# A fused RWKV and ELU-MLP kernel: a planner's order of work replaced by written-out lines for each engine

## The chip, the cores and the metric

The kernel runs on one core of a Trainium2 chip. A core has five engines that take their instructions in order, each from its own line, and wait for one another by semaphores: TensorE (PE in the profile; PEld is its weight load), VectorE (DVE), ScalarE (ACT), GpSimd (POOL) and SyncE (SP), which here only issues DMAs. The metric is the device time of one launch in microseconds (us), lower is better.

## The reference

For 4 batches and 8 heads of width 48 a state of 48x48 runs over 768 steps: the output row of a step is r_t (state + (u k_t) v_t), and then the state becomes w_t state + k_t v_t. The rows of all heads, 384 wide, 3072 of them, go through an MLP with a hidden width of 2048:

```python
for t in range(S):
    cur = np.einsum('bhd,bhe->bhde', u[None] * kt, vt)
    y[:, :, t] = np.einsum('bhd,bhde->bhe', rt, state + cur)
    state = wt[:, :, :, None] * state + np.einsum('bhd,bhe->bhde', kt, vt)
...
h = x @ w_in
g = np.where(h > 0.0, h, alpha * (np.exp(np.minimum(h, 0.0)) - 1.0))
return (g @ w_out).astype(np.float32)
```

## The kernel before, in words

**Attention.** The recurrence is cut into 24 units of 512 token rows over all heads (six chunks of four units). Units 0 to 3 hold 128 steps of one batch, the others 64 steps of two batches. A unit i is a set of tasks, named by a letter code and i:

- `ld_w`, `ld_k`, `ld_rk`, `ld_v`: its loads (SP). `es`, `gs` (L488, L497 and L498, VectorE): running products of the decays w. `rh` (L503): k and r times those. `rk`, `rku`, `md` (L510, L513, L517): the diagonal term. `sp` puts it into a mask tile `ams` (ScalarE L545, VectorE L550 or, from unit 8, GpSimd L556).
- `tr` (L590) transposes k on TensorE, `kt` (L636, ScalarE) copies it out. `s` (L590, L597) makes the scores in PSUM, `mk` (L626 to L632, VectorE) puts them into `ams`. `v` (L577, L648) makes the unit's output and its part of the state; from unit 8 (the stacked units) `v` runs first the scores of unit i + 1 (L597), then the state part (L648), then the outputs (L577, into py).
- `rc`, `tc`: four DMAs each that put r and the state into the tiles of a stacked unit (SP, L567 and L573). `xf`, `xh`, `xl`: the unit's output split into two fp32r halves. `up`, `sc` (L705, L640): update and scaling of the state. `fl` (L507, ScalarE) counts decays over 1 (for units 0 to 7 on a second load of w, `ld_wx`, into the one buffer `wx`); `pc` (L493) keeps the unit's product of decays. `least`, `guard`, `verdict` make a check of the two at the end.

**MLP.** The 16 slices f of the hidden width arrive as 64-bit floats and are converted once: `raw` (load), `a`, `cs` (ScalarE), `cb`, `cc` (VectorE L735, L739), `wh`, `wl` (L742 to L754, the two fp32r halves). For a chunk and a slice there is a step n (104 in all; numbers run through the chunks, 24 in the first, which also has steps of a quarter and half of the columns in plain fp32, then 16 in each): `g1.n` (TensorE, L303 or L299: 9 or 6 matmuls into `ph`), `r1.n`, `r2.n` (ScalarE L307, L310), `stt.n` (VectorE L313), `gh.n` (ScalarE L317), `gl.n` (VectorE L321), `g2.n` (TensorE, L334 or L331, into `acc`). `ph`, `m`, `gh` and `gl` have two buffers each. `out`, `store` bring out a chunk; at the end `g2a`, `part` and `end.0` to `end.3` do it in pieces.

**The order.** `Plan` holds each task with its engine, a duration (`COST`), the tasks it follows (`after`) and the buffers it takes (`hold`). `Plan.order` is a list scheduler: it steps through time and gives each free engine the ready task with the earliest due time, worked back from the due times of the chunks (`BEGINS`) and shifted by a table of amounts for single tasks (`NUDGE`); a task marked `lock` on VectorE or GpSimd isn't started while a locked one runs on the other engine. The tasks are then emitted in the planned order, which fixes each engine's line; at run time only semaphores hold an instruction back. Up to `g2.0` some matmuls on a tile of ones (`FILL`, L457) are put in front of named tasks.

Of the kernel before, what the change touches and what calls it, by code (L numbers as in the profile page):

```python
# [22 lines left out]
NC = S // C  # L23
# [20 lines left out]
DUE = {0: 9.0}  # L44
# [18 lines left out]
COST = dict(es=1.235, gs=1.47, pc=0.2, pd=0.9, md=0.165, spa=2.43, spd=0.685, rh=0.685, hat=1.22, rk=0.48, rku=0.48, prk=1.02, prku=1.02, dg=0.545, mk=0.74, mk0=1.4, up=0.545, upa=0.32,  # L63
            sc=0.6, xl=0.557, cand=0.555, cv=0.955, wl=0.952, stt=0.688, gl=0.69, fl=0.93, kt=0.522, xh=0.48, a=0.905, sg=2.0, la=0.913, wh=0.833, wg=0.83, r1=0.598, r2=0.632,
            gh=0.62, sp=1.95, s=1.62, s0=1.6, s8=0.82, tr=0.42, v=1.7, v0=1.6, v9=2.3, vs=0.47, vu=0.37, mk2=1.5, drc=300, dtc=300, g=2.04, g32=2.65, out=0.6)
# [10 lines left out]
FIRST = "ACT"  # L76
SPARE = (1,)
PAD = 32
RAW_AT = (1.6, 1.6)
LEAD = 110.0  # L80
# [1035 lines left out]
```

## Time and profile before

| | us |
|---|---|
| median of 3 runs | 503.06 (502.89 to 504.56) |
| the profiled execution | 502.57 |
| its span (first to last instruction) | 500.9 |
| TensorE busy | 488.9 (98%) |
| VectorE busy | 350.0 (70%) |
| ScalarE busy | 270.6 (54%) |
| GpSimd busy | 41.4 (8%) |

Busy is the time in which an engine has an instruction under way. Matmuls overlap, and the profile draws each longer than the distance to the next one, so a short stop of TensorE can lie under a drawn matmul.

### The profile page before, as it was taken

To read this page: it belongs to the slowest core of one execution; us is meant where nothing else is said; L and a number is where in the kernel's file an instruction comes from. 1 tells how busy PE (TensorE), PEld (TensorE's weight loads), DVE (VectorE), ACT (ScalarE), POOL (GpSimd) and SP (SyncE) were. 2 spreads that over 40 slices of the span, in tenths; PEclk is the share of its full clock that TensorE was granted. 3 is DMA by queue.
4 is the path that set the end of the run, shared out by engine and by line. 5 is a ranking of instruction groups with operands and counts; after the bars stand their busy time and mean duration, and the time that the engine had idled before them with its cause. 6 is when DMAs were issued, how large, how long until landed. Compare 5 with 4: busy or idle time off the path is not lost.

```text
span 500.9 us, 12029 instructions
## 1 busy us (share of the span) xinstructions
PE 488.9 (98%) x5014; PEld 403.0 (80%) x5014; DVE 350.0 (70%) x525; ACT 270.6 (54%) x526; POOL 41.4 (8%) x57
## 2 busy tenths in 40 slices
PE   9998999999999999998999999999999999999996
PEld 8986888777887888886887778878888878888885
DVE  7999999989998997444899463699564343333332
ACT  4986677656654635535565625437445253544542
POOL 2000000002233011010011020020111000000000
PEclk9999999999999999999999999999999999999999
DMA  8999266634624543335951427032430100010001
GB/s 272 348 286 299 61 227 190 213 94 112 195 50 111 146 130 92 118 92 132 210 151 50 142 64 198 22 106 84 109 100 6 28 3 1 0 65 0 1 0 67
DMA packets 45611, 57.27 MB, mean 114 GB/s; under 512 B 29168, under 2 KB 29296, under 8 KB 45552
## 3 DMA queue, kind: packets, MB, share of 16 engines
q1 hardware_dynamic: 45120, 55.66, 39.7%
q8 instruction: 41, 0.67, 0.6%
q10 hardware_dynamic: 432, 0.79, 0.4%
q14 instruction: 18, 0.15, 0.1%
HBM read 45.42 MB, written 4.72 MB: 100 GB/s over the span
## 4 chain that ended last, share of the span: by engine, by line
PE 62%; DVE 18%; DMA 10%; issue 4%; ACT 3%; SPq 2%; DVEq 0%; ACTq 0%
PE ph L303 27%; PE acc L334 25%; DMA wraw<-in_wraw_dram 5%; DMA wx<-in_wkr_dram 3%; PE acc L331 2%; DMA k<-in_wkr_dram 2%; DVE gl L321 2%; DVE m L313 2%; PE py L577 2%; DVE k L503 2%; PE ph L299 2%; DVE eg L488 2%; DVE ams L632 1%; PE px L597 1%; DVE w_l L754 1%
## 5 line engine op out<-in xcount | busy, mean ns | idle before, releaser
L313 DVE SCALAR_TENSOR_TENSOR m<-m,ph 128x512 f32<-128x512 f32 (+2 forms) x104 | 66.6, 641 | 74.7 <-ACT m L310 74.5
L303 PE MATMUL ph<-xh,w_l 128*128 128x512 f32 x270 | 105.5, 391 | 0.8 <-DVE w_l L754 0.8
L334 PE MATMUL acc<-gh,w_l 128*128 128x512 f32 x268 | 104.6, 390 | 0.0
L307 ACT ACTIVATE m<-ph 128x512 f32<-128x512 f32 (+2 forms) x104 | 58.4, 563 | 80.0 <-PE ph L303 65.3
L321 DVE TENSOR_TENSOR gl<-m,gh 128x512 fp32r<-128x512 f32 x90 | 62.2, 692 | 43.9 <-ACT gh L317 43.8
L317 ACT CAST gh<-m 128x512 fp32r<-128x512 f32 x90 | 55.6, 618 | 66.5 <-PE acc L334 40.0
L303 PE MATMUL ph<-xh,w_h 128*128 128x512 f32 x180 | 72.2, 401 | 1.2 <-DVE m L313 1.1
L334 PE MATMUL acc<-gl,w_h 128*128 128x512 f32 x180 | 70.5, 392 | 1.5 <-DVE gl L321 1.5
L334 PE MATMUL acc<-gh,w_h 128*128 128x512 f32 x180 | 71.7, 398 | 0.0
L303 PE MATMUL ph<-xl,w_h 128*128 128x512 f32 x180 | 70.2, 390 | 0.0
L310 ACT ACTIVATE m<-m 128x512 f32<-128x512 f32 (+2 forms) x104 | 62.1, 599 | 2.1
L303 PEld LDWEIGHTS ph<-xh,w_l 128*128 128x128 f32 x270 | 50.7, 188 | 12.0 <-DVE w_l L754 1.2
L334 PEld LDWEIGHTS acc<-gh,w_l 128*128 128x128 f32 x268 | 50.3, 188 | 10.4
L556 POOL TENSOR_SCALAR_AFFINE_SELECT ams<-md 64x512 f32<-64x512 f32 x32 | 28.4, 887 | 217.1 <-PE py L577 178.9
L334 PEld LDWEIGHTS acc<-gl,w_h 128*128 128x128 f32 x180 | 33.8, 188 | 9.4 <-DVE gl L321 2.8
L303 PEld LDWEIGHTS ph<-xh,w_h 128*128 128x128 f32 x180 | 33.8, 188 | 9.3 <-DVE m L313 1.6
L334 PEld LDWEIGHTS acc<-gh,w_h 128*128 128x128 f32 x180 | 33.8, 188 | 8.1 <-ACT gh L317 0.4
L303 PEld LDWEIGHTS ph<-xl,w_h 128*128 128x128 f32 x180 | 33.8, 188 | 6.5
L303 PE MATMUL ph<-xh,w_g 128*128 128x512 f32 x90 | 35.5, 394 | 0.5 <-DVE m L313 0.5
L303 PE MATMUL ph<-xl,w_g 128*128 128x512 f32 x90 | 35.0, 389 | 0.0
L334 PE MATMUL acc<-gh,w_g 128*128 128x512 f32 x88 | 34.9, 397 | 0.0
L334 PE MATMUL acc<-gl,w_g 128*128 128x512 f32 x88 | 34.6, 393 | 0.2
(121 smaller groups left out, 683.8 us busy)
## 6 DMA issues: line engine op xcount, KB each, us to landing
wraw<-in_wraw_dram SPq DMA_DIRECT2D x16, 768.0 KB, 9.7
k<-in_wkr_dram SPq DMA_DIRECT2D x24, 448.0 KB, 5.1
rk<-in_rk_dram SPq DMA_DIRECT2D x20, 384.0 KB, 4.3
w<-in_wkr_dram SPq DMA_DIRECT2D x24, 227.9 KB, 4.1
wide<-in_vp_dram SPq DMA_DIRECT2D x32, 128.0 KB, 3.6
out_dram<-o SPq DMA_DIRECT2D x15, 256.0 KB, 2.7
ams<-k SPq DMA_DIRECT2D x64, 48.0 KB, 2.4
wide<-st SPq DMA_DIRECT2D x64, 48.0 KB, 2.1
```

Source lines behind the costliest of these rows:

```text
L299: nc.tensor.matmul(ph, w_f[f][:, 0, k], x_[2][:, k], start=(k == 0), stop=(k == NK - 1))
L303: nc.tensor.matmul(ph, w[f][:, 0, k], y[:, k], start=(k == n == 0), stop=(k == NK - 1 and n == 2))
L307: act(s["m"], s["ph"], AF.Relu, scale=-1.0)
L310: act(s["m"], s["m"], AF.Exp, scale=-1.0)
L313: stt_(s["m"], s["m"], -1.0, s["ph"], ALU.add, ALU.max)
L317: nc.scalar.copy(s["gh"], s["m"])
L321: nc.vector.tensor_tensor(s["gl"], s["m"], s["gh"].bitcast(F32), ALU.subtract)
L331: nc.tensor.matmul(a_, w_f[f][:, 1, m], fold(s, s["m"][:, a:b]), start=first, stop=final)
L334: nc.tensor.matmul(a_, w[f][:, 1, m], fold(s, g[:, a:b]), start=(first and n == 0), stop=(final and n == 2))
L488: nc.vector.tensor_tensor_scan(out=eg[:, 0, 0:n][:, ::-1], data0=u_["w"][:, 1:n + 1][:, ::-1], data1=reset[:, 0, 0:n][:, ::-1], initial=0. ...
L503: tt(t, t, u_["eg"][:, :, 0:u_["n"]].rearrange("d z (s t) -> d z s t", t=u_["L"] + 1)[..., 1:], ALU.mult)
L556: nc.gpsimd.affine_select(out=am[rs, h].rearrange("t q p s -> t (q p) s"), in_=u_["md"][rs].rearrange("t q p -> t (q p)").unsqueeze(2).bro ...
```

## The change

`Plan.order` no longer chooses. `SEQUENCE` holds a written-out line of all tasks for each engine and for SP; `order` walks these lines with the task durations and merges them into one emission order. `NUDGE`, the due times and the locks go; some `COST` entries and load sizes are set anew, which now affects only how the lines are merged. The task `v` of a stacked unit becomes two: `va` (scores of the next unit and the state part) and `v` (the outputs); `mk` of the next unit and `up` follow `va`, and the bank px is given free after it. The instructions of all tasks stay. The diff, cut (all of PE's line, the start of the others):

```diff
-DUE = {0: 9.0}
...
-BEGINS = (21.0, 114.0, 191.0, 266.5, 342.0, 417.5, 483.5)
-SOON = 0.0
-SLACK = 1.0
-EARLY = 8.0
-STAG = 17.0
-STAG1 = 9.0
...
+SEQUENCE = dict(
+    PE="""
+pd.0 s.0 pd.1 s.1 v.0 v.1 g1.0 g1.1 pd.2 g1.2 g2.0 g1.3 g2.1 s.2 g2.2 g1.4 v.2 pd.3 g1.5 g2.3 g2.4 s.3 g1.6 g2.5 g1.7 v.3 g2.6 g1.8 g2.7 g1.9 g1.10
+g2.8 g1.11 g2.9 g1.12 g2.10 g1.13 g2.11 g1.14 g2.12 s.4 g2.13 g1.15 g1.16 v.4 g2.14 g1.17 g1.18 g2.15 g2.16 g1.19 s.5 g2.17 g1.20 v.5 g2.18 g2.19 s.6
+g1.21 v.6 g2.20 g1.22 s.7 g2.21 v.7 g1.23 g2.22 g1.24 g1.25 g2.23 g1.26 g1.27 g2.24 g2.25 g1.28 g1.29 g2.26 tr.8 g2.27 g1.30 s.8 g1.31 g2.28 g2.29
+va.8 v.8 g1.32 g1.33 tr.9 g2.30 g1.34 va.9 v.9 g2.31 g2.32 g2.33 g1.35 tr.10 g1.36 va.10 v.10 g2.34 g1.37 g2.35 tr.11 g1.38 g1.39 g2.36 va.11 v.11
+g2.37 g1.40 g1.41 tr.12 g2.38 g2.39 g1.42 va.12 v.12 g1.43 g2.40 tr.13 g2.41 g1.44 g1.45 g2.42 g2.43 g1.46 g2.44 g1.47 g1.48 g2.45 g1.49 va.13 v.13
+g2.46 g2.47 g1.50 tr.14 g2.48 va.14 v.14 g1.51 g1.52 g2.49 g1.53 tr.15 g2.50 g2.51 g1.54 g1.55 va.15 v.15 g2.52 g2.53 g1.56 g1.57 tr.16 g2.54 g2.55
+g1.58 va.16 v.16 g1.59 g2.56 g1.60 g2.57 tr.17 g1.61 g2.58 g1.62 va.17 v.17 g2.59 g2.60 g1.63 tr.18 g2.61 va.18 v.18 g1.64 g1.65 g2.62 tr.19 g2.63
+g1.66 g1.67 g2.64 g1.68 g2.65 g2.66 va.19 v.19 g1.69 g1.70 g2.67 g1.71 g2.68 g1.72 g2.69 g2.70 tr.20 g1.73 g2.71 g1.74 va.20 v.20 g1.75 g2.72 g2.73
+g1.76 g1.77 g2.74 g1.78 g2.75 g1.79 g2.76 g2.77 g1.80 g1.81 tr.21 g2.78 g1.82 g2.79 g2.80 g1.83 va.21 v.21 g2.81 g1.84 g2.82 g1.85 g2.83 g1.86 g1.87
+va.22 v.22 g2.84 v.23 g2.85 g1.88 g2.86 g2.87 g1.89 g1.90 g2.88 g1.91 g1.92 g2.89 g2.90 g1.93 g1.94 g2.91 g2.92 g1.95 g1.96 g2.93 g1.97 g2.94 g1.98
+g2.95 g1.99 g2.96 g2.97 g1.100 g1.101 g2.98 g2.99 g1.102 g1.103 g2.100 g2.101 g2a.0 guard g2a.1 g2a.2 g2.102 g2.103
+""",
+    DVE="""
+es.0 gs.0 rkc.0 es.1 rh.0 gs.1 rkc.1 mk.0 cb.2 rh.1 cc.2 cb.0 cc.0 mk.1 cb.1 cc.1 xl.0 cb.3 rkc.2 es.2 stt.0 gs.2 stt.1 rh.2 es.3 stt.2 cc.3 stt.3
+mk.2 gs.3 rkc.3 cb.6 cb.4 stt.4 rh.3 es.4 cc.4 cc.6 cb.5 stt.5 cc.5 mk.3 stt.6 wl.6 es.5 stt.7 cb.7 gs.4 cb.8 cc.7 stt.8 rk.5 cc.8 wl.7 stt.9 rk.4
+sc.4 rku.4 wl.8 stt.10 gs.5 md.4 xl.2 stt.11 xl.3 cb.9 rku.5 xl.1 stt.12 cc.9 sp.4 rh.4 cb.10 stt.13 md.5 cc.10 wl.9 stt.14 mk.4 rk.6 gl.14 wl.10 es.6
+cb.11 stt.15 cc.11 gs.6 stt.16 gl.15 sc.5 sp.5 xl.4 cb.12 rk.7 rku.6 cc.12 gl.16 wl.11 stt.17 rh.5 up.4 cb.13 md.6 stt.18 gl.17 wl.12 cc.13 stt.19
+rh.6 mk.5 sc.6 gl.18 wl.13 cb.14 gl.19 sp.6 cc.14 up.5 xl.5 rku.7 es.7 stt.20 md.7 mk.6 sp.7 gl.20 wl.14 gs.7 sc.7 xl.6 up.6 rh.7 stt.21 cb.15 gl.21
+cc.15 rk.8 mk.7 stt.22 wl.15 rku.8 gl.22 md.8 es.8 xl.7 gs.8 stt.23 up.7 es.9 rk.10 gl.23 rk.9 stt.24 rh.8 stt.25 rku.9 gl.24 sc.8 gl.25 es.10 wl.0
+gs.10 rku.10 stt.26 stt.27 sc.9 gl.26 gl.27 gs.9 md.10 md.9 stt.28 wl.2 wl.1 stt.29 gl.28 rk.11 gl.29 rh.9 mk.8 rh.10 stt.30 es.11 gs.11 wl.3 stt.31
+gl.30 gl.31 xl.8 up.8 sc.10 mk.9 stt.32 rk.12 es.12 gl.32 stt.33 rh.11 rku.12 gs.12 stt.34 rku.11 gl.33 wl.4 md.12 es.13 xl.9 md.11 up.9 wl.5 sc.11
+mk.10 gl.34 gs.13 stt.36 stt.35 gl.35 gl.36 rk.13 rk.14 xl.10 up.10 stt.37 sc.12 rku.14 rh.12 gl.37 mk.11 es.14 stt.38 rku.13 md.13 gs.14 md.14 xl.11
...
+    ACT="""
+pc.0 md.0 pc.1 sp.0 a.2 cs.2 kt.0 a.0 cs.0 md.1 sp.1 a.1 cs.1 kt.1 xf.0 up.0 xh.0 a.3 cs.3 r1.1 xf.1 up.1 r1.0 r2.0 md.2 r2.1 sp.2 r1.2 r1.3 r2.2 r2.3
+a.6 pc.3 kt.2 cs.6 a.4 cs.4 r1.4 xf.2 pc.2 up.2 r2.4 md.3 sp.3 cs.5 a.5 r1.5 r2.5 wh.6 kt.3 a.7 r1.6 r2.6 xh.2 cs.7 r1.7 r2.7 a.8 xf.3 cs.8 xh.1 r1.8
+r2.8 pc.4 wh.7 r1.9 r2.9 cs.9 wh.8 r1.10 xh.3 r2.10 cs.10 r1.11 r2.11 a.9 r1.12 r2.12 up.3 r1.13 a.10 r2.13 wh.9 r1.14 r2.14 pc.5 wh.10 gh.14 kt.4
+a.11 cs.11 r1.15 r2.15 r1.16 pc.6 r2.16 gh.15 cs.12 fl.0 xh.4 a.12 r1.17 gh.16 r2.17 wh.11 cs.13 r1.18 a.13 r2.18 wh.12 gh.17 gh.18 r1.19 r2.19 wh.13
+a.14 kt.5 gh.19 cs.14 xh.5 r1.20 cs.15 r2.20 fl.1 wh.14 pc.7 kt.6 gh.20 r1.21 xh.6 a.15 r2.21 gh.21 r1.22 r2.22 kt.7 wt.0 wh.15 gh.22 xh.7 r1.23 r2.23
...
+    SP="""
+ld_w.0 ld_k.0 ubd ld_w.1 raw.2 ld_k.1 raw.0 raw.1 ld_v.0 ld_v.1 raw.3 ld_k.2 ld_w.2 ld_w.3 ld_v.2 raw.6 raw.4 ld_k.3 ld_v.3 ld_w.4 raw.5 raw.7 ld_w.5
+raw.8 ld_rk.4 raw.9 ld_rk.5 ub raw.10 ld_k.4 ld_v.4 ld_w.6 ld_rk.6 ld_k.5 raw.11 ld_rk.7 ld_v.6 raw.12 ld_wx.0 raw.13 ld_k.6 ld_v.5 ld_v.8 ld_k.7
+raw.14 ld_w.7 ld_wx.1 ld_v.7 raw.15 ld_w.8 ld_rk.8 ld_wx.2 ld_v.9 ld_w.9 ld_k.8 ld_rk.9 ld_rk.10 ld_w.10 tc.8 ld_k.9 ld_k.10 ld_v.10 ld_w.12 ld_rk.11
...
+        line = {e: [tuple(int(x) if x.isdigit() else x for x in k.split(".")) for k in s.split()] for e, s in SEQUENCE.items()}
+        assert sorted(map(str, ts)) == sorted(str(k) for s in line.values() for k in s)
+        assert all(ts[k]["eng"] == e for e, s in line.items() for k in s)
+        place = {k: n for s in line.values() for n, k in enumerate(s)}
+        waits = {k: [(d, True) for d in t["after"] if d in ts] for k, t in ts.items()}
+        pools = {}
+        for k, hs in self.holds.items():
+            for p, us in hs:
+                pools.setdefault(p, []).append((k, us))
+        for p, hs in pools.items():
+            rank = {k: n for n, k in enumerate(self.queue[p])} if p in self.queue else place
+            hs.sort(key=lambda h: rank[h[0]])
+            for (k, us), (after, _) in zip(hs, hs[SLOTS[p]:]):
+                waits[after] += [(u, False) for u in set(us) | {k} if u != after]
+        free = {e: 0.0 for e in line}
+        server, lanes, ended, order = DMA_FIRST, [0.0] * DMA_LANES, {}, []
         while len(order) < len(ts):
+            best = None
+            for e, s in line.items():
+                if not s or any(d not in ended for d, _ in waits[s[0]]):
                     continue
+                t = ts[s[0]]
+                start = max([free[e], t["start"]] + [ended[d] + (LAT + DRAIN * (real and ts[d]["eng"] == "PE") if ts[d]["eng"] != e else SELF * (real and e not in ("PE", "SP")))
+                                                     for d, real in waits[s[0]]])
                 if e == "SP":
+                    start = max(start, lanes[t["lanes"] - 1])
+                if best is None or start < best[0]:
+                    best = start, e
+            assert best, ("stuck", {e: s[:1] for e, s in line.items()})
+            start, e = best
+            t = ts[line[e].pop(0)]
+            end = start + t["dur"]
+            free[e] = end - NEXT[e]
+            if e == "SP":
+                server = max(server, end) + t["size"] / DMA_RATE
+                end = server + DMA_LAT + t["lands"]
+                lanes = sorted(lanes[t["lanes"]:] + [end] * t["lanes"])
+            t["began"], t["ended"] = start, end
+            ended[t["key"]] = end
+            order.append(t)
+        return order
...
-    def stacked(u_):
-        i, w = u_["i"], u_["stack"]
-        ahead = i + 1 < NU
-        if ahead:
-            scores(units[i + 1], halves(), close=u_["last"])
+    def ahead(u_):
+        if u_["i"] + 1 < NU:
+            scores(units[u_["i"] + 1], halves(), close=u_["last"])
         if not u_["last"]:
             u_["pu"] = px[0:R2, 0:2, NP * L:NP * L + NP * D].rearrange("d h (p e) -> d h p e", p=NP)
-            update_part(u_, [w[:, h] for h in range(2)], start=False, stop=NP - 1)
+            update_part(u_, [u_["stack"][:, h] for h in range(2)], start=False, stop=NP - 1)
+
+    def stacked(u_):
+        w = u_["stack"]
         u_["py"] = py[:, 0:2 * NK * L].rearrange("d (h k t) -> d h k t", h=2, k=NK)
...
+                add(("tr", i), "PE", K["tr"], lambda u_=u_: transposes(u_), [("rh", i)] + [("xl", i - 1), ("xh", i - 1)] * (i > STACK))
+        add(("mk", i), "DVE", K["mk0" if u_["whole"] else "mk2" if new else "mk"], lambda u_=u_: mask(u_), [("s", i) if own else ("va", i - 1), ("sp", i)])
...
-        cost = K["v9"] - K["vu"] * u_["last"] - K["vs"] * (i == NU - 1) if new else K["v0" if u_["whole"] else "v"]
-        add(("v", i), "PE", cost, lambda u_=u_, fn=stacked if new else value: fn(u_), after,
-            due=BEGINS[c] - (B - 1 - i % B) * (STAG if c > 1 else STAG1) - 2.0 if c else None, slack=SLACK * new)
+        cost = K["v0"] if u_["whole"] else K["v"]
+        if new:
+            cost = K["v9"] - K["va"]
+            if i + 1 < NU:
+                add(("va", i), "PE", K["va"] - K["vu"] * u_["last"], lambda u_=u_: ahead(u_), after)
+                after = [("va", i)]
+        add(("v", i), "PE", cost, lambda u_=u_, fn=stacked if new else value: fn(u_), after)
...
-            add(("up", i), FIRST if u_["whole"] else "DVE", K["upa" if u_["whole"] else "up"], lambda u_=u_: update(u_), [("xf" if u_["whole"] else "xh", i)])
+            add(("up", i), FIRST if u_["whole"] else "DVE", K["upa" if u_["whole"] else "up"], lambda u_=u_: update(u_), [("xf", i) if u_["whole"] else ("va" if new else "xh", i)])
...
-            hold("pa", ("v", i), [("up", i), ("mk", i + 1)], fifo=False)
+            hold("pa", ("va", i), [("up", i), ("mk", i + 1)], fifo=False)
```

## Rows read from the trace of the kernel before

**Rows 1.** The page, busy time of each engine, share of the span and instructions

```profile
PE 488.9 (98%) x5014; PEld 403.0 (80%) x5014; DVE 350.0 (70%) x525; ACT 270.6 (54%) x526; POOL 41.4 (8%) x57
```

**Rows 2.** Stretches: length, busy us of each engine, clock, DMA share, GB/s

```profile
core 0: us, PE busy (x) PEld busy (x) DVE busy (x) ACT busy (x) POOL busy (x), PEclk, DMA share, GB/s
0.00:25.00 25.00, 23.92 (x264) 22.66 (x265) 21.79 (x33) 17.88 (x45) 3.32 (x14) 1.00 0.95 310
25.00:64.00 39.00, 36.65 (x296) 31.73 (x295) 38.60 (x58) 27.65 (x67) 1.60 (x3) 1.00 0.73 208
64.00:160.00 96.00, 93.95 (x1404) 75.61 (x1403) 91.56 (x134) 61.38 (x109) 16.71 (x16) 1.00 0.53 154
...
225.00:235.00 10.00, 8.46 (x36) 5.91 (x35) 5.46 (x9) 6.26 (x13) 0.00 (x0) 1.00 0.38 88
235.00:345.00 110.00, 108.86 (x1077) 88.83 (x1076) 79.44 (x118) 56.24 (x113) 9.46 (x10) 1.00 0.48 124
345.00:497.00 152.00, 152.00 (x1179) 124.73 (x1177) 65.07 (x103) 69.31 (x119) 3.93 (x6) 1.00 0.10 28
```

**Rows 3.** Waits of PE: whom for, us in total, times, longest us

```profile
PE px L577 <- ACT kt L636: 2.3, 1, 2.3
PE ph L303 <- DVE m L313: 1.6, 4, 0.5
PE acc L334 <- DVE gl L321: 1.5, 2, 1.2
...
PE ph L303 <- DVE w_l L754: 0.8, 1, 0.8
```

**Rows 4.** Timeline of PE, unit 3 and two pairs of fp32 steps

```profile
39.18 1.16 PE L597 MATMUL px<-k 48*128 48x128 f32 x16
42.60 1.08 PE L577 MATMUL px<-ams,wide 128*32 128x128 f32 x32 [2.27 <-ACT kt L636]
...
45.51 2.75 PE L299 MATMUL ph<-wide,w_f 128*128 128x256 f32 x12
48.10 2.75 PE L331 MATMUL acc<-m,w_f 128*128 128x256 f32 x12
```

**Rows 5.** Timeline of PE around two stops

```profile
113.00 0.39 PE L303 MATMUL ph<-xh,w_h 128*128 128x512 f32 x1
113.23 0.39 PE L303 MATMUL ph<-xl,w_h 128*128 128x512 f32 x1
114.44 0.50 PE L303 MATMUL ph<-xh,w_l 128*128 128x512 f32 x1 [0.82 <-DVE w_l L754]
...
227.19 0.50 PE L334 MATMUL acc<-gl,w_h 128*128 128x512 f32 x1 [1.23 <-DVE gl L321]
```

**Rows 6.** The tile wx: its instructions, and what its engine sat idle for

```profile
L507 ACT ACTIVATE wx<-wx,lim x8: 723/728/733, 217.8 to 261.7; 112x516 f32<-112x516 f32 x4, 112x520 f32<-112x520 f32 x4
...
  DMA wx<-in_wkr_dram: 13.9, 7
```

**Rows 7.** VectorE's groups of one shape, 0 to 191.2 us

```profile
L503 DVE TENSOR_TENSOR k<-k,eg 112x1024 f32<-112x1024 f32 x14 | 17.6, 1254 | 0.3 <-DMA k<-in_wkr_dram 0.3
L313 DVE SCALAR_TENSOR_TENSOR m<-m,ph 128x512 f32<-128x512 f32 x25 | 16.8, 677 | 0.5 <-ACT m L310 0.5
...
L488 DVE TENSOR_TENSOR_SCAN eg<-w,reset 112x520 f32<-112x520 f32 x12 | 15.4, 1286 | 0.0
L498 DVE TENSOR_TENSOR_SCAN eg<-w,reset 112x520 f32<-112x520 f32 x12 | 15.3, 1274 | 0.4
...
L513 DVE TENSOR_TENSOR rk<-rk,ub 128x384 f32<-128x384 f32 x12 | 6.5, 550 | 0.0
L510 DVE TENSOR_TENSOR rk<-rk 128x384 f32<-128x384 f32 x12 | 6.5, 554 | 0.0
L517 DVE TENSOR_REDUCE md<-rk 128x8 f32<-128x384 f32 x11 | 5.9, 547 | 0.0
```

**Rows 8.** Timeline of VectorE and GpSimd at a meeting of the two

```profile
138.60 1.03 POOL L750 CAST w_g<-wt 128x768 fp32r<-128x768 f32 x1 [4.90 <-DVE w_l L754]
138.85 1.87 DVE L488 TENSOR_TENSOR_SCAN eg<-w,reset 112x520 f32<-112x520 f32 x1
```

More of the change, by code (lines that the diff above doesn't have):

```diff
@@ L178, in order @@
-        users = {}
-        ring = {p: [0, [False] * n] for p, n in SLOTS.items()}
-        free = lambda p, n: not any(ring[p][1][(ring[p][0] + x) % len(ring[p][1])] for x in range(n))
-        ready = {e: [] for e in ("PE", "DVE", "ACT", "POOL", "SP")}
-        count = {k: len(t["after"]) for k, t in ts.items()}
-        at = {k: t["start"] for k, t in ts.items()}
-        rank = {k: n for n, k in enumerate(ts)}
-        busy = {e: 0.0 for e in ready}
-        locked = {"DVE": 0.0, "POOL": 0.0}
@@ L187, in order @@
-        server, lanes = DMA_FIRST, [0.0] * DMA_LANES
-        turn = {p: list(q) for p, q in self.queue.items()}
-        for k in ts:
-            if not count[k]:
-                ready[ts[k]["eng"]].append(k)
-        after = lambda a, b: LAT + (DRAIN if a == "PE" else 0.0) if a != b else 0.0 if a in ("PE", "SP") else SELF
-        events, now, order = [], 0.0, []
+        line = {e: [tuple(int(x) if x.isdigit() else x for x in k.split(".")) for k in s.split()] for e, s in SEQUENCE.items()}
@@ L786, in rwkv_elu_kernel @@
             if n == "rk" and DIAG[i] == "PE":
                 continue
-            add(("ld_" + n, i), "SP", DMA_ISSUE, lambda u_=u_, n=n: load(u_, n), start=early, size=kb)
+            two = n == "v" and i >= STACK
+            add(("ld_" + n, i), "SP", DMA_ISSUE + 0.75 * two, lambda u_=u_, n=n: load(u_, n), size=kb, lanes=1 + two, lands=LANDS[n] if i >= B else 0.0)
         again = i > 0 and units[i - 1]["whole"] != u_["whole"]
         if again:
-            add(("reset", i), "POOL", 1.2, lambda u_=u_: set_reset(nc.gpsimd, u_), [("gs", i - 1)], lock=True)
@@ L888, in rwkv_elu_kernel @@
                 add(("gh", n), "ACT", K["gh"] * (part + 0.4) / 1.4, lambda s=s, fns=fns: fns["gh"](s), [("stt", n)])
-                add(("gl", n), "DVE", K["gl"] * (part + 0.2) / 1.2, lambda s=s, fns=fns: fns["gl"](s), [("gh", n)], lock=True)
-            before, due = [("stt" if full else "gl", n), ("g2", n - 1)], t + pace * part * 2 + g
+                add(("gl", n), "DVE", K["gl"] * (part + 0.2) / 1.2, lambda s=s, fns=fns: fns["gl"](s), [("gh", n)])
+            before = [("stt" if full else "gl", n), ("g2", n - 1)]
             if c == NC - 1 and final:
@@ L904, in rwkv_elu_kernel @@
-                add(("g2", n), "PE", g * 2 / 3 * (1 - CUT / N), lambda x=x, y=y: rest(x, y, b, single, "b"), [("g2", n - 1)], due=due)
-                add(("end", 0), "ACT", K["out"], lambda fns=fns: fns["end"](0), [("g2a", 1)], due=due)
-                add(("end", 1), "DVE", K["out"], lambda fns=fns: fns["end"](1), [("g2a", 2)], due=due)
-                add(("end", 2), "DVE", K["out"] * CUT / N, lambda fns=fns: fns["end"](2, a, last["a"]), [("g2", n - 1), ("part",)], due=due)
-                add(("end", 3), "DVE", K["out"] * (1 - CUT / N), lambda fns=fns: fns["end"](2, b, last["b"]), [("g2", n), ("part",)], due=due)
+                add(("part",), "ACT", K["out"], fns["partial"], [("g2", n - 2)])
@@ L909, in rwkv_elu_kernel @@
+                add(("end", 0), "ACT", K["out"], lambda fns=fns: fns["end"](0), [("g2a", 1)])
+                add(("end", 1), "DVE", K["out"], lambda fns=fns: fns["end"](1), [("g2a", 2)])
+                add(("end", 2), "DVE", K["out"] * CUT / N, lambda fns=fns: fns["end"](2, a, last["a"]), [("g2", n - 1), ("part",)])
+                add(("end", 3), "DVE", K["out"] * (1 - CUT / N), lambda fns=fns: fns["end"](2, b, last["b"]), [("g2", n), ("part",), ("end", 2)])
                 hold("pa", ("g2", n - 1), [("end", 2)], fifo=False)
@@ L911, in rwkv_elu_kernel @@
             elif not (c == NC - 1 and (f, lo, hi) == steps[c][-2]):
[L912 removed]
+                add(("g2", n), "PE", g, lambda s=s, fns=fns: fns["g2"](s), before)
             prior = s
```

273 lines of the change are left out of this document (85 added, 188 removed).

## The prediction

> **What bounds the kernel now.** I read the busy line of the page first, then a table of stretches, then TensorE's own waits, then for each stretch with idle time the engine that was late. The busy line [rows 1] shows TensorE (PE) at 488.9 of 500.9 us: the kernel is TensorE-bound and 12.0 us of its span are without a matmul. No schedule can give more than those, since the change adds and removes no matmul. The table of stretches [rows 2] says where they lie (length less PE busy): 1.08 us in 0 to 25 us, 2.35 in 25 to 64, 2.05 in 64 to 160, 1.54 in 225 to 235, 1.14 in 235 to 345, none in 345 to 497, and the rest behind the last matmul. The granted clock is at its full level (2.4 GHz) in every one of these stretches, so no part of the time is a clock's. The middle four make 7.1 us.
>
> TensorE's waits [rows 3] name the late engines: one wait of 2.3 us for ScalarE's copy of a transposed k (`kt`), four for VectorE's `stt` (1.6 in all), two for its `gl` (1.5), one for a `wl` (0.8); two smaller ones are left out. These 8 waits are 6.2 of the 7.1 us.
>
> Recorded idle understates a stop. In an undisturbed run matmuls of 512 columns start 0.23 us apart though each is drawn 0.39 long [rows 5]; before the wait for `wl` the starts are 1.21 us apart, so 0.98 us was lost where 0.82 is booked. Some 0.16 us hide in each stop: ten stops make 1.6. **Ceiling:** 7.1 + 1.6 = 8.7 us for a schedule that never stops TensorE between 25 and 497 us.
>
> **The change, part by part.** The instructions are the same in number and form. New are the order in each engine's line (and in SP's line of DMAs), and so which wait stands in front of which work. Every engine takes its line in order, so a wait holds all that is behind it.
>
> A, 25 to 64 us. Before, `v.3` (L577, then L648) follows `s.3` directly: `s.3` is drawn to 39.18 + 1.16 = 40.34, `v.3` starts at 42.60, 2.27 idle [rows 4], since `kt.3` and `mk.3` must come in between. The new PE line has `g1.6 g2.5 g1.7` between `s.3` and `v.3`. A pair of such tasks takes 48.10 - 45.51 = 2.59 us [rows 4], so three take 3.9 and cover the 2.27, if the weights of f = 4 and 5 are converted by then; the new DVE line has `cc.4` and `cc.5` ahead of `mk.3`, as it must. In this stretch VectorE is busy 38.60 of 39.00 us [rows 2], so not all of it can come back. Of 2.35 + 0.16 I take **2.2**; ends 0 (VectorE late instead) and 2.5.
>
> B, 64 to 160 us. VectorE is busy 91.56 of 96.00 us [rows 2]: nearly a second bound. The gain must come from taking work off it that is not yet due. I counted one place: up to `stt.38` (the 39th of L313; 25 + 10 + 4 of them by 191.2 us, the smaller two shapes not shown) the kernel before has run 12 + 4 of the scans `es` (4 of a smaller shape not shown), and the `gs`, `rh`, `rk`, `rku`, `md` of [rows 7]. In the new line fewer stand ahead of `stt.38`: 1 `es`, 2 `gs`, 1 `rh`, 1 `rk`, 2 `rku`, 2 `md` fewer and nothing more. That is 1.29 + 2 x 1.27 + 1.25 + 0.55 + 2 x 0.55 + 2 x 0.55 = 7.8 us less VectorE work [rows 7], while the PE line has two more g1 tasks ahead of `g2.38` (`g1.40 g1.41`: 18 matmuls of 0.23 = 4.1 us of cover). The late units are put off: `v.20` to `v.23` stand behind more g1 and g2 tasks than before, where VectorE is half idle. Against it: ahead of `stt.20` the new line has more VectorE tasks than the old one, so the early part of this stretch gets no relief. Of 2.05 + 4 x 0.16 = 2.7 I take **1.3**; ends -4.4 (the second rival) and 2.7.
>
> C, 225 to 235 us. ScalarE runs the flags `fl.0` to `fl.7` of the first eight units late, all between 217 and 262 us, each on its own load into one buffer (`wx`), and sits idle 13.9 us in front of seven of them [rows 6]. Behind it in its line wait `gh`, so `gl` on VectorE, so TensorE: the stop of 1.23 us at 227.19 [rows 5]. The new lines spread the eight: `ld_wx.0` is issued behind `raw.12`, `fl.0` comes behind `cs.12`, and so on to `fl.7` in the fifth chunk, each several tasks after its load. Of 1.54 + 2 x 0.16 = 1.9 I take **1.7**; ends 0 (the waits go along to other places) and 1.9.
>
> D, 235 to 345 us. Here VectorE is 72% busy [rows 2], and the stops come from order alone: the old line runs `mk`, `xl`, `up`, `sc` of a unit as a block ahead of an `stt` that TensorE waits for. The new line strews them among `stt` and `gl`. Of 1.14 + 3 x 0.16 = 1.6 I take **0.9**; ends 0 and 1.6.
>
> The split of a unit's TensorE task into `va` and `v`: in all but the last unit the new PE line has `va.i` directly ahead of `v.i`, so the matmuls stand as before. What it changes is that the schedule counts `mk`, `up` and the bank px as free after `va`. I cost it at nothing; VectorE's slack of part B hides a `mk` that comes earlier, and without that slack it would cost one `mk`. The head to 25 us has the same PE line in both kernels up to `g1.4 v.2`: nothing. The tail: `guard` and `verdict` move to the last tasks, in front of `end.1`, and `part` moves behind `end.0`; all wait for the last matmuls anyway: nothing, and at worst one ScalarE copy of 0.6. SP's line is mixed anew (loads of `w` and `rk` earlier, stores between other DMAs); its prices are those of A and C, a load that comes late, with the same ends.
>
> **Sum.** 2.2 + 1.3 + 1.7 + 0.9 = 6.1 us. The profiled execution took 502.57 us (span 500.9 and 1.67 around it), so 496.5; it lies 0.49 under the median of the runs, 503.06, so the forecast is **497.0**. With every stop gone it would be 503.06 - 8.7 = 494.4.
>
> **Rivals.** *Late units (slower).* A stored line places `tr`, `va`, `v` of each of the 16 stacked units at a fixed point among g1 and g2. If a unit's chain (`sc`, four state DMAs, `mk`, `kt`) is late on the chip, TensorE stands still, as it did for `kt` in [rows 4]: 2.27 + 0.16 = 2.4 us each. Tight spots are, among others, `tr.10 g1.36 va.10`, `tr.14 g2.48 va.14` and `v.22 g2.84 v.23`, with one task between. From 497.0, one late unit gives 499.4, two 501.8, four 506.6; with four or more it is slower than before beyond a measurement's reach. For: the old plan, too, had placed every unit without a stop and had them on the chip. Against: of the old stops just one was a unit's, and most units now have more tasks in front of them.
>
> *The port clash (most of the gain lost).* The old planner never let a GpSimd task and a locked VectorE task run together; the new one drops this. In the trace a scan that met a GpSimd cast took 1.87 us [rows 8] where the mean of the scan is 1.29 [rows 7]; 0.58 us more. In 64 to 160 us there are 16 GpSimd instructions [rows 2]; if 15 of them each cost VectorE that, it is 8.7 us, of which its idle 4.4 hides half: 4.4 us later, 501.4. For: VectorE is full there. Against: the old trace shows the clash despite the planner's care, so that care did not decide it, and the new line's slack ahead of `stt.38` is 7.8. The Trainium skill, page "SBUF — State Buffer", section "SBUF: two separate sides", has the shared port pair of VectorE and GpSimd as an exclusive lock held for a whole instruction; by that rule this rival is the outcome where the two meet often, and the row of 1.87 us agrees with it.
>
> *The same stops elsewhere (no change).* A fixed order is as blind to what the chip does late as a planned one, and 7 us in 500 is little: old stops go and as many of 0.3 to 1 us come, at `cc.4` in A and behind `xl.11` and `xl.23`, where chunks 2 and 5 begin one g2 task after the unit they need. 503.
>
> **How the numbers follow.** A measurement of this kernel tells a change from none at about 0.3%, 1.5 us. Forecast (495 to 499.5) 0.54, port clash or another partial loss (499.5 to 501.5) 0.17, no change 0.14, slower by late units 0.15. So faster 0.71, same 0.14, slower 0.15. The low end is the ceiling with 0.4 for runs that scatter, 494.0; the high end takes in the partial losses, no change and half of one late unit's step above it, 503.6, which leaves out most of the slower case.
>
> **What would show it.** Right: PE busy 488 to 490 us in a span near 495; PE's idle in 25 to 64 us under 0.5; no PE wait on `kt` above 1 us; ScalarE's idle for `wx` under 5 us in place of 13.9; `stt.38` with VectorE work 7 to 8 us lighter. Wrong: PE waits of 1 us or more on `mk`, `kt` or `px` in front of L577 (late units), scans of 1.6 us and more in 100 to 160 us in numbers (port clash), or a PE busy time that grew, which would mean the matmuls themselves run otherwise.

## The result and the profile after

The changed kernel takes 496.07 us (median of 4 runs, 495.5 to 496.78), where the kernel before took 502.98 beside it: ratio 0.9864, interval 0.9828 to 0.9901. The profiled execution took 496.44 with a span of 494.7. The forecast was 497.0, range 494.0 to 503.6. Four executions at a lower granted clock are left out of all ratios here: one of `again` (690 us, clock 0.655), one of `oldAC` (512) and two of the kernel before (509 and 510).

The busy line of the page after, which answers to [rows 1], and the chain that ended last by engine (before: PE 62%, DVE 18%, DMA 10%):

```profile
PE 485.8 (98%) x5014; PEld 402.3 (81%) x5014; DVE 351.0 (71%) x525; ACT 265.0 (54%) x526; POOL 40.9 (8%) x57
...
PE 89%; DVE 5%; ACT 3%; issue 1%; DMA 1%; DVEq 0%; ACTq 0%
```

TensorE is now 89% of the chain: nearly all of the time that remains is its own work. The stretches after, columns as in [rows 2]:

```profile
0.00:25.00 25.00, 22.80 (x259) 21.14 (x260) 21.60 (x33) 17.05 (x43) 3.30 (x14) 1.00 0.95 314
25.00:64.00 39.00, 39.00 (x309) 33.71 (x308) 38.48 (x59) 30.88 (x71) 1.59 (x3) 1.00 0.67 222
64.00:160.00 96.00, 93.80 (x1285) 75.53 (x1284) 89.34 (x129) 61.61 (x114) 12.98 (x12) 1.00 0.49 139
...
225.00:235.00 10.00, 10.00 (x112) 8.15 (x114) 5.19 (x7) 5.15 (x11) 0.00 (x0) 1.00 0.52 132
235.00:345.00 110.00, 110.00 (x1265) 90.69 (x1265) 79.33 (x118) 51.55 (x104) 10.96 (x12) 1.00 0.42 111
```

The second column is the length, the third what TensorE was busy. Three stretches of four have no idle left: 25 to 64, 225 to 235 and 235 to 345 us. The stretch from 64 to 160 still has 2.2 us, about as much as before (2.05). TensorE's waits after, all four that the profile books, which answer to [rows 3]:

```profile
PE px L529 <- issue: 1.2, 1, 1.2
PE py L479 <- DVE rkc L474: 1.1, 2, 0.6
PE acc L409 <- POOL ones L377: 1.1, 1, 1.1
PE ph L255 <- DVE m L265: 0.9, 2, 0.6
```

The wait of 2.3 us for `kt`, both for `gl` and the one for `wl` are gone. New is a wait called issue: nothing that the profile shows held TensorE there. Its timeline after at `v.7`, where that wait is, and at `v.3`, which answers to [rows 4]:

```profile
43.40 1.08 PE L529 MATMUL px<-ams,wide 128*32 128x128 f32 x32
...
111.15 0.46 PE L529 MATMUL px<-k,st 48*32 48x64 f32 x24
112.79 0.31 PE L529 MATMUL px<-k,st 48*32 48x64 f32 x6 [1.17 <-issue]
```

`v.3` starts without a wait. `v.7` ends with 32 small matmuls of one kind, and 26 of them have run when it stops. By starts that stop is 1.38 us.

Idle understates a stop, so I also add up, matmul by matmul, the distance to the next start less the usual distance for the same three neighbouring shapes (their median over the runs of this case). That is time lost by TensorE, worked out from both traces:

| us | 0 to 27 | 27 to 64 | 64 to 165 | 165 to 225 | 225 to 345 | behind 345 | behind the last matmul's start |
|---|---|---|---|---|---|---|---|
| before | 4.1 | 3.9 | 8.0 | 3.4 | 9.1 | 3.8 | 4.1 |
| after | 4.6 | 1.2 | 8.2 | 2.6 | 5.9 | 2.7 | 4.8 |
| gain | -0.5 | 2.7 | -0.3 | 0.8 | 3.1 | 1.1 | -0.7 |

The gains sum to 6.2 us, and the spans differ by 6.2. Single columns scatter: the run `oldorder` below has the lines of before, and by the same measure it lost 6.5 us in 64 to 165 and 3.9 in 165 to 225.

### The profile page after: what moved, and what is told of

Same layout as the page of the kernel before. It is cut to its first block, busy times and chain, and to the rows that moved or that the text cites. A ratio compares the mean times of both kernels' runs of the same rounds, so it can differ in the third digit from the quotient of the medians.

```text
span 494.7 us, 12041 instructions
## 1 busy us (share of the span) xinstructions
PE 485.8 (98%) x5014; PEld 402.3 (81%) x5014; DVE 351.0 (71%) x525; ACT 265.0 (54%) x526; POOL 40.9 (8%) x57
## 4 chain that ended last, share of the span: by engine, by line
PE 89%; DVE 5%; ACT 3%; issue 1%; DMA 1%; DVEq 0%; ACTq 0%
PE acc L286 36%; PE ph L255 36%; PE acc L283 3%; PE py L529 3%; PE ph L251 3%; PE px L549 3%; PE px L529 2%; PE px L600 2%; PE py L542 1%; ACT ams L497 1%; DVE gl L273 1%; ACT w_f L673 1%; ACT wraw L678 1%; PE py L479 1%; DVE k L455 1%
## 5 line engine op out<-in xcount | busy, mean ns | idle before, releaser
L273 DVE TENSOR_TENSOR gl<-m,gh 128x512 fp32r<-128x512 f32 x90 | 64.1, 717 | 50.0 <-ACT gh L269 49.5
L262 ACT ACTIVATE m<-m 128x512 f32<-128x512 f32 (+2 forms) x104 | 61.1, 598 | 1.4
L508 POOL TENSOR_SCALAR_AFFINE_SELECT ams<-md 64x512 f32<-64x512 f32 x32 | 27.4, 858 | 217.3 <-DVE md L469 117.8
```

The source lines that it names most:

```text
L262: act(s["m"], s["m"], AF.Exp, scale=-1.0)
L273: nc.vector.tensor_tensor(s["gl"], s["m"], s["gh"].bitcast(F32), ALU.subtract)
L508: nc.gpsimd.affine_select(out=am[rs, h].rearrange("t q p s -> t (q p) s"), in_=u_["md"][rs].rearrange("t q p -> t (q p)").unsqueeze(2).bro ...
```

## The experiments

The theory behind all of them: the change is worth what the four stretches of the prediction won by their order, and nothing else of it counts.

### Is it the order alone?

`oldorder` stores the lines that the old planner made in the new tables and joins `va` and `v` again. `fused` keeps the new lines and only joins the two tasks.

```diff
-        add(("v", i), "PE", cost, lambda u_=u_, fn=stacked if new else value: fn(u_), after)
+        add(("v", i), "PE", cost, lambda u_=u_, fn=both if new else value: fn(u_), after)
...
+    def both(u_):
+        ahead(u_)
+        stacked(u_)
```

> The lines of the kernel before, task for task, written into the new kernel's tables (va and v as one task again). Theory, all of the gain is the order in the lines: 503 us, ratio to the kernel before within 0.3% of 1, TensorE's idle again 2.4 us in 25 to 64 us and about 14 us of ScalarE idle in front of the loads of wx. Rival, the merging or the split of the task is worth something by itself: 501 or less.

> The new lines, but va and v of a unit are one task again, and mk of the next unit and up follow it. The lines and the instructions of each engine stay. Theory, the split costs and gives nothing on the chip, since a semaphore hangs on the last matmul that writes what is read: 496 us, within 1 us of the changed kernel. Rival, the split lets mk and up start earlier: 498 or more, with waits of mk (L584) on the unit's last matmuls in py.

`oldorder`: 502.15 us, ratio 1.0003 (0.9983 to 1.0022). In its trace every engine has the same instructions in the same order as in that of the kernel before. The three largest of TensorE's waits in [rows 3] are there again; the one for `wl` is not:

```profile
PE px L529 <- ACT kt L588: 2.0, 1, 2.0
PE acc L286 <- DVE gl L273: 1.5, 2, 1.2
PE ph L255 <- DVE m L265: 1.5, 4, 0.5
```

`fused`: 496.5 us, ratio 0.9882 (0.9857 to 0.9907), whose interval overlaps the changed kernel's. So neither the new bookkeeping nor the split, taken alone, costs or brings anything that shows. The split had a use when the lines were laid out: with `up` tied to `xh` as before, the joined task closes a ring of waits in the new lines, so in `fused` `up` follows `v`. The profiled execution of `fused`, 500.35 us, is the longest of its five. It has a stop at 23.85 us that the others lack; what it is comes out under `v7late`:

```profile
PE acc L600 <- issue: 1.8, 1, 1.8
```

### Part A, the place of v.3

`undoA` moves one task of the changed kernel back: `v.3` right behind `s.3`. `oldA` is the mirror: the old lines with `v.3` moved to where it may hide its wait.

```diff
 undoA (lines of the changed kernel, PE)
-... g2.4 s.3 g1.6 g2.5 g1.7 v.3 g2.6 ...
+... g2.4 s.3 v.3 g1.6 g2.5 g1.7 g2.6 ...
 oldA (lines of the kernel before, PE)
-... g2.4 s.3 v.3 g2.5 g1.7 g1.8 ...
+... g2.4 s.3 g2.5 g1.7 v.3 g1.8 ...
```

> The changed kernel with v.3 put back right behind s.3 in TensorE's line; all else stays. Theory, part A of the gain is this one place: 2.3 us more, 498.4, with one wait of about 2.3 us in front of v.3 (L529) near 40 us. Rival, VectorE sets the pace up to 64 us, so that the stop is given back before the first fp32r step: 496 to 497.

> The lines of before with one thing of the change alone: in TensorE's line v.3 stands behind g2.5 and g1.7 in place of right behind s.3. Theory (the prediction's sum: what is won at 42 us is kept to the end): the stop of 2.2 us at 42 us goes and nothing comes in its place, 500.0 us against 502.2 for the lines of before. Rival (the stretch behind it is held by VectorE, whose line is unchanged, so that the time won at 42 us is waited for again before 130 us): stops in 64 to 130 us grow by 1.5 us or more, 501.7 us or more.

`undoA`: 503.48 us, ratio 1.0017 (1.0002 to 1.0031). One move back lost the whole gain, three times what was expected. TensorE's timeline and the stretch:

```profile
38.27 1.16 PE L549 MATMUL px<-k 48*128 48x128 f32 x16
42.96 1.93 PE L529 MATMUL px<-ams,wide 128*32 128x128 f32 x32 [3.52 <-issue]
44.82 0.88 PE L600 MATMUL px<-wide,kt 128*48 128x48 f32 x16
45.63 2.93 PE L251 MATMUL ph<-wide,w_f 128*128 128x256 f32 x6
...
53.41 1.56 PE L251 MATMUL ph<-wide,w_f 128*128 128x256 f32 x6 [0.78 <-ACT wide L653]
```

```profile
25.00:64.00 39.00, 34.70 (x278) 29.91 (x277) 31.54 (x47) 26.34 (x62) 1.08 (x2) 0.91 0.50 167
```

Three things add up. The stop is longer than before (3.8 us by starts, before 2.5), since in the new lines `mk.3` stands further back on VectorE:

```profile
41.54 1.32 DVE L578 COPY_PREDICATED ams<-upper,px 128x512 f32<-128x512 uint32 x2
```

It ends at 42.86, and `v.3` starts 0.10 later: "issue" here hides a wait for `mk`. Then the granted clock falls: six matmuls that take 1.56 us at 53.41 take 2.93 at 45.63, and the stretch has 0.91. And the pause ran on through ScalarE, so that the matmuls at 53.41 waited 0.78 us for `xf.3`. By the table's measure the stretch lost 7.2 us more than in the changed kernel.

`oldA`: 505.01 us, ratio 1.0029 (0.9999 to 1.0058). Nothing won. But the rival had the wrong place too: the wait did not return in 64 to 130 us, it was not left at all.

```profile
42.97 1.88 PE L283 MATMUL acc<-m,w_f 128*128 128x256 f32 x6 [2.21 <-DVE m L265]
44.64 2.77 PE L251 MATMUL ph<-wide,w_f 128*128 128x256 f32 x6
...
41.28 1.34 DVE L578 COPY_PREDICATED ams<-upper,px 128x512 f32<-128x512 uint32 x2
42.50 0.41 DVE L265 SCALAR_TENSOR_TENSOR m<-m,ph 128x256 f32<-128x256 f32 x1
```

`g2.5` needs `stt.5`, and the old VectorE line has `stt.5` (42.50) behind `mk.3` (41.28). Behind `s.3` stood nothing that was ready. So A is not the move of `v.3` by itself: it takes VectorE's line too, in which `stt.5` stands ahead of `mk.3`. Without the move (`undoA`) the gain is gone, and the move without VectorE's line (`oldA`) wins nothing. No run puts the two halves alone into the old lines.

### Part C, the flags on one buffer

`undoC` bunches `fl.0` to `fl.7` and their loads again, in the changed kernel. `oldC` spreads them in the old lines, nothing else moved. `oldAC` is `oldA` and `oldC` together.

```diff
 undoC (ACT; SP likewise: ld_wx.0 to ld_wx.4 ahead of rc.14)
-... cs.12 fl.0 xh.4 ...
+... r2.44 fl.0 fl.1 gh.43 fl.2 ... gh.46 fl.3 fl.4 ... r1.50 fl.5 ... gh.51 fl.6 ... r1.53 fl.7 ...
 oldC (ACT; SP: ld_wx.0 behind raw.12, ld_wx.1 behind raw.14, ... ld_wx.7 behind ld_rk.20)
-... r2.44 fl.0 kt.13 fl.1 xh.13 gh.43 fl.2 ...
+... r2.18 fl.0 r1.19 ... r2.21 fl.1 gh.21 ... gh.24 fl.2 ... r2.68 fl.7 ...
```

> The changed kernel with the eight flags fl.0 to fl.7 put back close together in ScalarE's line (between r2.44 and r2.53) and their loads into one buffer close together in SP's line. Theory, part C is this bunching: ScalarE idle in front of wx 10 us or more, TensorE stops of 1.5 to 3 us in that stretch, 498 us. Rival, the stops at 225 to 235 us had another cause: 496 to 496.7 although ScalarE waits for wx.

> The lines of before, with one thing of the change alone: the eight flags fl.0 to fl.7 and the eight loads into wx are spread from step 18 to step 69 in place of steps 44 to 53. Theory (the flags on one wx buffer held ScalarE and through gh the TensorE at 227 us): the stop of 1.2 to 1.5 us at 226 to 227 goes, the wx idle of 13.9 us goes, the kt and DVE stops of 64 to 160 us stay; 500.3 us against 502.2 for the lines of before as they are. Rival (the stop at 227 us has another cause, or spreading the loads sets other loads late): 502 us or more.

> The lines of before with v.3 moved as in the run oldA and the flags and wx loads spread as in the run oldC. Theory (the parts add up): 498.1 us, that is 2.2 and 1.9 less than the lines of before (502.2). Rival (the gain at 42 us is given back behind it): 499.8 us, no less than the flags alone.

`undoC`: 519.71 us, ratio 1.0343 (1.0315 to 1.0371). The tile `wx` and TensorE's first wait in it:

```profile
  DMA wx<-in_wkr_dram: 22.0, 6
...
PE acc L286 <- ACT gh L269: 12.5, 1, 12.5
```

The direction is the theory's, the size is not: my edit also put `rc.14` and other loads behind five loads that wait for one another, so the run shows that this place can stop TensorE for 12.5 us, not what the flags alone cost.

`oldC`: 500.03 us, ratio 0.9961 (0.993 to 0.9993), 1.96 us less by the ratio (0.4 to 3.5 by its interval), as the theory had it. Its own stretch:

```profile
225.00:235.00 10.00, 10.00 (x87) 8.26 (x77) 6.10 (x10) 5.46 (x10) 1.31 (x2) 1.00 0.54 140
```

TensorE is busy all 10 us where [rows 2] has 8.46, and no idle time in front of a flag is left. The cause of the stop at 227 us is thus shown. But the profiled execution, at 504.4 us one of the longest of the twelve, also paid elsewhere:

```profile
100.78 1.13 PE L549 MATMUL px<-k 48*64 48x64 f32 x32 [3.04 <-DVE xl L654]
102.45 0.79 PE L255 MATMUL ph<-xh,w_h 128*128 128x512 f32 x1
103.04 0.63 PE L255 MATMUL ph<-xl,w_h 128*128 128x512 f32 x1
...
100.00:130.00 30.00, 29.22 (x479) 23.62 (x480) 27.62 (x41) 16.72 (x33) 3.76 (x4) 0.89 0.44 111
```

`raw.14` landed some 3 us later than in `oldorder` (ScalarE began on it at 95.03 in place of 91.55), with `ld_wx.1` now issued right behind it; VectorE's conversion, then `xl`, then TensorE followed, and the clock fell on top. That the two loads held each other up is read from their order; no run tests it. `oldAC`, 505.4 us, ratio 0.9996 (0.9967 to 1.0024), has both faults: the stop at 42.8 us and one of 2.5 at 103.4. The sum of the parts, 498.1 of 502.2, would be a ratio of 0.992, so it was missed by some 4 us. In the old lines the moves do not add up.

### What is left: 64 to 165 us and the head

In 64 to 165 us nothing was won, and three stops of 0.5, 0.2 and 0.8 us at 153.9 to 159.7 are new. VectorE and GpSimd shortly ahead of them, in the changed kernel:

```profile
140.62 2.72 POOL L703 CAST w_g<-wt 128x768 fp32r<-128x768 f32 x2 [10.45 <-DVE w_l L707]
...
142.57 1.17 DVE L462 TENSOR_TENSOR rk<-rk 128x384 f32<-128x384 f32 x1
143.30 2.02 POOL L508 TENSOR_SCALAR_AFFINE_SELECT ams<-md 64x512 f32<-64x512 f32 x2
143.67 1.13 DVE L273 TENSOR_TENSOR gl<-m,gh 128x512 fp32r<-128x512 f32 x1
144.72 1.67 DVE L455 TENSOR_TENSOR k<-k,eg 112x1024 f32<-112x1024 f32 x1
```

In [rows 7] `rk` takes 0.55 us and `k` 1.25; `gl` has a mean of 0.69 in the kernel before. Counting each VectorE instruction that overlaps a GpSimd one and is 0.2 us or more over its form's median, before has 5 with 2.4 us of excess in all, after has 12 with 4.2 us. Each of the 12 began inside a GpSimd instruction and is longer by what was left of that one, less some 0.15 us: `rk` at 142.57 had 0.76 us of a cast left and took 0.62 more. All 12 read two operands from SBUF; the `stt`, which reads one from PSUM, keeps its 0.68 beside a cast. That agrees with the Trainium skill, page "SBUF — State Buffer", section "SBUF: two separate sides", by which such a VectorE instruction and a GpSimd one that reads SBUF shut each other out for a whole instruction, and whichever starts first goes first.

Three edits of the changed kernel, each against one stop that is left, then all three together, and the changed kernel once more beside them:

```diff
 castsACT (wh.0 to wh.5 from GpSimd's line into ScalarE's)
-nc.gpsimd.tensor_copy(w_h[f], raws[f][1].bitcast(F32))
+nc.scalar.copy(w_h[f], raws[f][1].bitcast(F32))
 v7late (PE)
-... s.7 g2.21 v.7 g1.23 g2.22 ...
+... s.7 g2.21 g1.23 v.7 g2.22 ...
 head (DVE)
-... xl.0 cb.3 rkc.2 es.2 ...
+... xl.0 rkc.2 cb.3 es.2 ...
```

> The changed kernel with six of GpSimd's tasks (wh.0 to wh.5, two copies each, at 128 to 162 us) given to ScalarE. Theory (VectorE's instructions are lengthened while GpSimd runs one, and that is what ate the gain of 64 to 160 us): of 12 lengthened VectorE instructions about half are left, the stops of 1.5 us at 153.9 to 159.7 us fall under 0.5, 494.9 us. Rival (VectorE is late there by its order alone, or ScalarE's extra 6 x 1.5 us makes gh late instead): 496 us or more.

> The changed kernel with v.7 moved behind g1.23 in TensorE's line, as it stood before; all else stays. Theory (the stop of 1.2 to 1.5 us in the middle of v.7, for which no wait is shown, comes from the many small matmuls of s.7, g2.21's last and v.7 following each other closely, so that the engine's queue runs out of instructions): the stop goes or falls under 0.4 us, 494.9 us. Rival (the stop sits at this place in the program for another reason): it stays, 496.1 us.

> The changed kernel with rkc.2 ahead of cb.3 in VectorE's line, as it stood before. Theory (the stop of 0.8 us at 23 us, which before did not have, is s.2 waiting for rkc.2 behind the copy cb.3): g1.2 ends 0.5 us earlier, 495.6 us. Rival (raw slice 3 is the next limit, so cb.3 put back costs what rkc.2 gains): 496.1 us.

> The changed kernel with three edits together: wh.0 to wh.5 on ScalarE, v.7 behind g1.23, rkc.2 ahead of cb.3. Theory (each stop that is left has its own cause): of the stops at 23.3 (0.8), 112.8 (1.4) and 153.9 to 159.7 us (1.5) none stays, 3.2 us less by start times with some 0.5 us of that eaten by smaller ones, 493.3 us. Rival (they only pass the wait on to the next place): 495.4 us, no less than with wh on ScalarE alone.

> The changed kernel once more, beside the others on one chip, to compare the three edits with. Theory: 496.1 us, the same stops, that of v.7 among them. Rival for the stop in v.7 (it depends on when the instructions happen to be fetched): 0.5 to 1.4 us of it may be missing.

| | us | ratio to before |
|---|---|---|
| castsACT | 495.41 | 0.9853 (0.9817 to 0.989) |
| v7late | 496.01 | 0.9872 (0.9833 to 0.9911) |
| head | 496.44 | 0.9878 (0.9841 to 0.9915) |
| combo | 493.9 | 0.9792 (0.976 to 0.9824) |
| again | 497.51 | 0.9861 (0.9828 to 0.9893) |

*castsACT.* The same instructions have their own durations again, and of the stops at 153.9 to 159.7 one of 0.2 us is left:

```profile
142.84 0.55 DVE L461 TENSOR_TENSOR rk<-rk 128x384 f32<-128x384 f32 x1
143.31 0.69 DVE L272 TENSOR_TENSOR gl<-m,gh 128x512 fp32r<-128x512 f32 x1
143.91 1.22 DVE L454 TENSOR_TENSOR k<-k,eg 112x1024 f32<-112x1024 f32 x1
...
130.00:165.00 35.00, 34.96 (x423) 28.23 (x422) 29.68 (x44) 23.02 (x44) 3.17 (x4) 1.00 0.49 131
```

In the changed kernel that stretch has TensorE busy 33.97, so 1.0 us came back; lengthened instructions are down to 5 (1.4 us). By the traces the clash is the cause. The time, 495.41 us, lies between the theory's 494.9 and the rival's 496, and its ratio doesn't tell this kernel from the changed one.

*v7late.* With `v.7` one task later it runs through, all 30 remaining matmuls in a row:

```profile
113.94 0.54 PE L529 MATMUL px<-k,st 48*32 48x64 f32 x30
```

The time shows nothing of it: 496.01 us is the rival's number, not the theory's 494.9, and the ratio is that of the changed kernel within its interval. So the stop's cause rests on the traces.

What holds `v.7` is seen among the DMAs. The profile's third part counts a queue of its own for instructions, with 41 packets of 16 KB:

```profile
q8 instruction: 41, 0.67, 0.6%
```

In the changed kernel one such packet is under way from 110.18 to 111.36 us; TensorE stops at 111.4 and goes on at 112.79. Seven traces have eight such stops: one each in the changed kernel's two, `undoA`, `undoC`, `castsACT` and `oldA` (there in `v.6`), and two in `fused`, that at 23.85 us among them. Each time a packet lands within 0.6 us of the stop's beginning, and work goes on 1.2 to 1.5 us after that landing. The places settle it. TensorE has 10133 recorded instructions, weight loads included, in the changed kernel, some 250 for each of the 41 packets. Ahead of the stops 449, 2241 or 3009 of them have run (3010 in `undoA`): 2241 is 449 and 7 x 256, 3009 is 449 and 10 x 256. And the packets that landed just then are the 1st, the 8th and the 11th. So a stop stands where a packet's first instruction is due, and TensorE's instructions come late. In all 14 traces no instruction at one of these places, 256 apart, starts sooner than 1.2 us after its packet's landing.

Some 200 small matmuls (`s.7`, `v.7`) stand close together there and are soon used up. In `v7late` the instruction at that place starts 3.4 us after the landing at 110.63, in `combo` 4.2. In `head`, where `v.7` stands as in the changed kernel, the packet came earlier, from 109.25 on, the distance was 1.7 us and there was no stop. What starts such a packet isn't shown.

*head.* `pd.2` starts without a wait, but in that execution two waits of 0.5 and 1.1 us stood earlier, at 13.3 and 16.4 us, in front of unit 1, whose line nobody had changed. The head's timing scatters by more than the 0.5 us in question; alone the edit shows nothing.

*combo* beats both kernels: in the same series its executions took 493.5 to 494.6 us, those of `again` that count 497.2 to 497.9. The stops at 23.3 and 112.8 us and those at 153.9 to 159.7 are gone; the largest left is 0.35 us. Its waits of TensorE:

```profile
PE acc L408 <- POOL ones L376: 1.1, 1, 1.1
PE ph L254 <- DVE w_l L706: 0.2, 1, 0.2
```

The first is the start of the program. So these stops did not pass their wait on, and by the traces each had its own cause, as the theory had it; by their times the three edits show only together.

## Why the prediction held, point by point

- **Ceiling and total.** The forecast of 497.0 stood 0.9 us above the result; the sum of 6.1 us compares with 6.2 between the spans. But terms failed on both sides and met in the middle, so the nearness of the total is in part luck. The ceiling of 494.4 was too high: the profiled execution of `combo` took 493.53, with gaps won back that are too small to be booked as idle. One sign of being right failed: TensorE is busy 485.8 us, not 488 to 490; the number of matmuls is the same, 5014.
- **"No part of the time is a clock's": true of the profiled execution only.** Beside `again`, 8 executions of the kernel before with a mean granted clock of 0.998 or more took 500.8 to 502.9 us, and 14 with 0.991 to 0.997 took 503.7 to 506.6. Nine of the changed kernel's ten have 0.997 or more. So part of the measured ratio looks like clock that the kernel before loses in some executions; its one trace has no such fall, so where isn't shown.
- **A, 2.2 us: right, by a wider change than named.** No wait on `kt`, idle of 0.0 in 25 to 64 us (forecast under 0.5), 2.7 us won in 27 to 64, a little over the step's upper end of 2.5. The step named the place of `v.3`; `undoA` and `oldA` show that the place of `stt.5` and `mk.3` on VectorE is the other half of it.
- **B, 1.3 us: wrong, -0.3.** Against `oldorder` it is -1.7. The lighter line of VectorE ahead of the 39th `stt` is there, to the instruction: 15 `es` where 16 stood, 14 `gs` for 16, 13 `rh` for 14, 11 `rk` for 12, 10 `rku` for 12, 9 `md` for 11; it starts at 188.63 us, before at 191.19. But the step took that for what decides this stretch. The old stops did go, the last of them at 157.5 us; two others took their place: `v.7`, which waits for no engine (1.4 us), and the clash with GpSimd (1.5 us). Without them (`combo`) this stretch has 0.2 us of idle in 64 to 160.
- **C and D, 1.7 + 0.9 us: right, 3.1 won together.** ScalarE's idle for `wx` is 0 (forecast under 5, before 13.9). `oldC` shows C by itself at 2 us. By the table's measure, cut at 237 us, C won 1.9 and D 1.3. D was sized too low: 0.9 of 1.6 was taken, and no idle is left in 235 to 345. No run changes D's part of the lines by itself, so its cause, the strewn block, stays argued.
- **Costed at nothing: the split, the head, the tail.** The split: right (`fused`). The head lost 0.5, since `rkc.2` now stands behind `cb.3`; the step looked at TensorE's line only. From the last matmul's start to the end it is 4.8 us for 4.1; over all runs here this piece goes from 4.1 to 6.1 with no order to it, so no cause is claimed.
- **Not in the sum:** 0.8 us in 165 to 225 and 1.1 behind 345, in gaps too small to be booked as idle. No run here takes them apart.
- **Late units:** not seen; no wait on `kt` or `xl` in the changed kernel. The nearest thing in the runs is `v.3` in `undoA`: it cost not 2.4 us but the whole gain, as the clock fell too.
- **Port clash:** real, as a part and not as the whole. It cost 1.5 us, not 4.4: over the whole span 12 VectorE instructions were lengthened, by 0.2 to 0.6 us each, 5 of them in this stretch, not 15 by 0.58. Those 5 are `rk`, `gl` and `k`; the scans that the rival named as its sign took at most 1.46 us anywhere.
- **Same stops elsewhere:** for B that is what happened.

## What to carry to other kernels

In a kernel that one engine bounds, count what its stops cost and who was late for each; a new order is worth just that. Judge a move with the lines of the other engines beside it: `v.3` alone moved in the old lines won nothing, moved back in the new ones it lost everything. When a planner's rule is dropped, look for what it had kept out: here the old lines, made under the lock between VectorE and GpSimd, had 5 lengthened VectorE instructions and the new ones 12. Six copies on ScalarE, which had room, brought 1.0 us of TensorE's idle back.

## What the runs showed of the hardware that was not expected

- **A stop can cost TensorE's clock as well.** In the kernel before, a stop of 2.5 us (by starts) at 42.6 us left the granted clock at 1.00. In `oldA` one of 2.5 at 43.0, in front of other work, was followed by six matmuls in 2.77 us in place of 1.56, and 25 to 64 us had 0.96; with one of 3.8 us in `undoA` it had 0.91, with one of 3.3 in `oldC` 100 to 130 us had 0.89. In between the level is the lower of two, 1.2 of 2.4 GHz: in `oldC` starts are 0.43 us apart where 0.23 is usual. Why two stops of one length differ isn't settled here.
- **TensorE can run out of instructions** while every operand is there: eight stops of 1.1 to 2.0 us by starts in seven traces, shown as "issue", each at the first instruction of a 16 KB packet.
- **A VectorE instruction with two SBUF operands that begins inside a GpSimd one can wait nearly to its end:** 12 in the changed kernel, 0.2 to 0.6 us longer each.
- **"issue" can also hide a wait** for another engine: in `undoA` `mk.3` ended 0.10 us ahead of the start.
